# Softmax reciprocals of two batches taken once per head and spread by TensorE, in a fused attention and feed-forward kernel

## The chip, the core and the metric

The kernel runs on one core of a Trainium2 chip. A core has TensorE (PE in the profile; PEld is its loading of weights), VectorE (DVE), ScalarE (ACT), GpSimd (POOL) and SyncE (SP), each with its own instruction queue, and 16 DMA engines. Each queue runs in order. The metric is the device time of one execution in microseconds (us). Before the change the median of four runs is 249.94 us (248.99 to 250.69).

## The reference

The first half is Nyström attention over 8 batches and 8 heads, with 576 positions, 64 values per head and 32 landmarks (means over 18 positions). Three softmaxes are formed, the middle one is inverted by six steps of an iteration, and the product goes with v. The second half is a feed-forward layer with silu on the 4608 x 512 result.

```python
A  = sm(q, k_lm)          # 576 x 32 per head, each row divided by its sum
Bm = sm(q_lm, k_lm)       # 32 x 32
C  = sm(q_lm, k)          # 32 x 576
Z  = Bm.transpose(...) / (norms of Bm)
for _ in range(6):
    Z = 2 * Z - Z @ Bm @ Z
x  = A @ Z @ C @ v        # then heads side by side: 4608 x 512
h  = x @ w_in             # 512 -> 2048
out = (h * sigmoid(h)) @ w_out
```

## The kernel before

All work is cut into named operations ("A.1" is the product for softmax A of batch 1), each with its possible engines, an estimated duration, what it depends on, a priority and the number of PSUM banks it takes. A list scheduler (`Plan.run`) places them on the engines by these estimates; the instructions are then written out in that order and every engine runs its own list as it stands. The table `ORDER` shifts the priority of single operations. `margin` (0.4 us in general, `Plan.MARGIN`) is how long after its inputs are expected a PE operation is placed. In the first 45 us PE gets filler matmuls on a zero tile `zer` wherever the plan has nothing for it.

Heads stand in two groups g of four, with 4 x 32 landmarks on the 128 partitions, and positions in two halves c of 288. For one batch b:

- k and q are loaded (POOL queue), transposed (`tr`, by PE for batches 0 to 2, by DMA from SP for the others) and copied to `qT`; landmark sums (`lms`, `lm`, `lmT`), the small softmax (`sb`, `pb`) and the iteration (`f0`, six pairs `ns` on PE and `nsd` on DVE, tile `st`) follow.
- C: product C, Exp `Cx` on ACT with the row sums, transposes `ct`, product with v (`cv`), scaled `wsb`, then `zt`.
- m: `m0` to `m3`, the product of `zt` with a quarter (chunk) of `w_in` each, copied to `m`. So `w_in` is applied before A.
- A: product A into four banks; Exp (L786) to the bf16 tile `et`, 128 landmarks by 288 positions for each g and c; then the row sums. A matmul with `hmask` (`bones`, S) sums each head's 32 partitions and puts the sum on all 32. ACT takes Ln of it from PSUM (L796, four of 288 columns) and then Exp of minus that, in place (L800, two of 576 columns). DVE multiplies `et` with this reciprocal to `etn` (L805, two of 576).
- Layer 1 (`h0` to `h15`, and `hx0`, `hx8` for the last positions): product of `m` with `etn`, silu on ACT to `gm` and `gx`.
- Layer 2: `p1` to `p7`, a product scheme with seven instead of eight partial products, with sums on DVE; PSUM results are copied or added into `ost` by ACT and DVE (`c11`, `c12`, `c21`, `c22`) and stored by `os` operations.

ACT has two tables, one with Exp and Ln and one with silu; a switch is an instruction of its own. All table operations of one batch's softmaxes form a group, and silu is held back while a group is open. Silu of batch 0 also needs `pb` of batch 1, so the groups of batches 0 and 1 come before the first silu. C.1 and A.1 wait for `etn` of batch 0.

A tile of the result leaves in four stores of 64 KB, all on SP; only the last pair of tiles is split over SP and ACT, its second tile in halves of 256 columns.

Of the kernel before, what the change touches and what calls it, by code (L numbers as in the profile page):

```python
# [7 lines left out]
FP = mybir.dt.float32  # L8
# [8 lines left out]


ORDER = {
    "tr09.0": (11.858, 0), "f0.0": (2417.6, 0), "nsd20.0": (1178, 0), "stf1.0": (616.27, 0),  # L20
    "ns51.0": (572.47, 0), "A.0": (-14.244, 0), "Ax10.0": (-14.785, 0), "S10.0": (429.53, 0),
    "Ln10.0": (-9.5622, 0), "etn1.0": (303.1, 0), "mc00.0": (-3617.7, 0), "mc30.0": (2226.2, 0),
    "tr10.1": (11.49, 0), "trc09.1": (-0.41208, 0), "tr014.1": (4003.2, 0), "lms110.1": (600, 0),
    "lms1112.1": (182.03, 0), "lms006.1": (4219.8, 0), "ns00.1": (-205.63, 0),
    "Ax10.1": (-68.603, 0), "Ln10.1": (-2.9831, 0), "Ax11.1": (-215.55, 0),
    "Ln11.1": (-2436.1, 0), "Rs1.1": (-229.25, 0), "Cx00.1": (3739.9, 0), "ctc10.1": (-135.78, 0),
    "trc014.2": (-5.8828, 0), "Ln10.2": (-1553.1, 0), "Cx10.2": (-2.3811, 0), "h11.1": (3839, 0),
    "c12@5100.0": (-2978.9, 0), "A.3": (-178.57, 0), "cv0.3": (-11.245, 0), "h2.2": (332.83, 0),
    "h3.2": (185.78, 0), "h4.2": (18.041, 0), "h11.2": (452.76, 0), "h15.2": (51.328, 0),
    "p5@5200.0": (-179, 0), "c21@5200.0": (912.94, 0), "A.4": (-26.98, 0), "Ln00.4": (288.73, 0),  # L30
    "h11.3": (169.04, 0), "ss00@5320.0": (-3259.3, 0), "p5@5340.0": (-0.29183, 0),
    "p7@5340.0": (-4146.8, 0), "p3@5340.0": (212.88, 0), "nsd00.5": (-245.94, 0),
    "S10.5": (-942.67, 0), "p7@5420.0": (-0.18573, 0), "ns40.6": (267.98, 0),
    "ss00@5500.0": (-5226.2, 0), "cv0.7": (-3352.4, 0), "wrc.7": (1720.5, 0),
    "p5@5620.0": (-0.51334, 0), "p7@5700.0": (-1.908, 0), "p4@5720.0": (524.17, 0),
    "p2@5740.0": (15.37, 0),
}


# [264 lines left out]
def act_us(n):  # L304
    return 0.06 + 0.00083 * n
# [11 lines left out]
def kernel(  # L317
# [24 lines left out]
    SW = 128 + L  # L342
    NPE = 2
    NTR = 3
    SBF = 2
    MERGE = False
    WM = False
    NCT = 2
# [11 lines left out]
    def bank(o, i=0):  # L360
        return banks[o.slot[i]]
# [169 lines left out]
    def folds(e):  # L531
        for r in (0, 64):
            for c in (0, 64):
                nc.vector.tensor_copy(out=fold[r:r + 64, c:c + 64], in_=idb[r:r + 64, r:r + 64])
    cfold = A("fold", [("DVE", 0.6)], folds, [cid], 90.0)


# [6 lines left out]
    def attn(b):  # L544
# [225 lines left out]
        def am(e):  # L770
            for g in range(NG):
                for h in range(4):
# [5 lines left out]
                    lmT_all + ([] if cr else [(pb_op, -0.2)]) + qt_ops[0, 0] + qt_ops[0, 1] + ready, p0 + 20,  # L778
                    psum=4, tiled="q")
        me["A"].opens = grp  # L780
        for g in range(NG):
            et, ln = et_r[g], ln_r[g]
            lns = []
            for c in range(2):
                x = A(f"Ax{g}{c}.{b}", [("ACT", act_us(HS))],
                      lambda e, g=g, et=et, c=c: nc.scalar.activation(  # L786
                          out=et[:, c], in_=bank(me["A"], 2 * g + c)[:, 0:HS], func=AF.Exp,
                          scale=sc / J),
                      [me["A"], prev.get(f"etn{g}")], p0 + 21 + g, table="exp",
                      group=grp).reads(me["A"], 2 * g + c)  # L790
                me["S", g, c] = A(f"S{g}{c}.{b}", [("PE", mm_us(HS))],
                                  lambda e, g=g, c=c, et=et: mm(
                    bank(me["S", g, c])[:, 0:HS], bones, et[:, c]), [x, c0],
                    p0 + 22 + g, psum=1)
                lns.append(A(f"Ln{g}{c}.{b}", [("ACT", act_us(HS))],
                             lambda e, g=g, c=c, ln=ln: nc.scalar.activation(  # L796
                                 out=ln[:, c], in_=bank(me["S", g, c])[:, 0:HS], func=AF.Ln),
                             [me["S", g, c]], p0 + 25 + g, table="exp", group=grp).reads(
                                 me["S", g, c]))
            x = A(f"Rs{g}.{b}", [("ACT", act_us(S))], lambda e, ln=ln: nc.scalar.activation(  # L800
                out=ln, in_=ln, func=AF.Exp, scale=-1.0), lns, p0 + 25.1 + g, table="exp",
                group=grp)

            def etm(e, g=g, et=et, ln=ln):
                nc.vector.tensor_tensor(out=etn[:, g, :], in0=et.rearrange("p c x -> p (c x)"),  # L805
                                        in1=ln.rearrange("p c x -> p (c x)"), op=OP.mult)
            me[f"etn{g}"] = A(f"etn{g}.{b}", [("DVE", dve_us(S))], etm,
                              [x, l1_done.get(b - 2)], p0 + 30)
# [184 lines left out]
    def layer2_plain(gm, c, deps, places, prio):  # L993

        pieces = []
        for h in range(2):
            cell = {}
            cols = slice(c + 128 * h, c + 128 * h + 128)
            for qt in range(4):
                def f(e, qt=qt, cell=cell, cols=cols):  # L1000
                    for dc in range(4 * qt, 4 * qt + 4):
                        mm(bank(cell["o"]), gm[:, dc, cols], w_out_sb[:, dc, :], start=(dc == 0),
                           stop=(dc == NDC - 1))
                d = deps(4 * qt, 4 * qt + 4) + [wo_ops[qt]]
                o = A(f"o{qt}@{prio + h}", [("PE", mm_us(512, 4))], f,
                      d + ([(pieces[-1], 0.0)] if qt else []), prio + h + 0.01 * qt,
                      psum=0 if qt else 1, cls="L2")
                cell.setdefault("o", o)
                pieces.append(o)
            i = nost[0] % 6  # L1010
            nost[0] += 1
            t = ost_r[i]
            a = A(f"oc@{prio + h}", either(512), lambda e, t=t, cell=cell: copy(
                e, t, bank(cell["o"])), [pieces[-1]] + ost_st.get(i, []),
                500.0 + prio / 100).reads(cell["o"])
            ost_st[i] = [A(f"os@{prio + h}", [("SP", 2.2)],
                           lambda e, t=t, h=h: [store(e, t, places[h], m) for m in range(4)],
                           [a], prio, dma=0.65, lag=3.5)]
        return pieces
# [4 lines left out]
            out=out[b * S:(b + 1) * S, cols].rearrange("(l j) n -> j l n", j=J)[j],  # L1024
            in_=t[L * m:L * m + L, cols])

    def layer2_pair(gm, c, deps, places, prio, parts=1, spread=False):

        n = npair[0]
        npair[0] += 1  # L1030
# [74 lines left out]
        ss_last[n] = [p3, p5, p6]  # L1105

        for i, t, h, dep in ((lo_i, lo_t, 0, [c11, c12]), (hi_i, hi_t, 1, [c21, c22])):
            if spread and h:
                ost_st[i] = [A(f"os{u}{m}@{prio + h}", [("SP", 0.45), ("ACT", 0.45)],
                               lambda e, m=m, t=t, u=u: store(e, t, places[1], m, slice(  # L1110
                                   HM * u, HM * u + HM)), [dep[u]], prio + 0.1 * u,
                               dma=0.1, lag=1.5) for u in range(2) for m in range(4)]
            elif spread:
                ost_st[i] = [A(f"os{m}@{prio}", [("SP", 0.45), ("ACT", 0.45)],
                               lambda e, m=m, t=t: store(e, t, places[0], m), dep, prio,
                               dma=0.1, lag=1.5) for m in range(4)]
            else:
                ost_st[i] = [A(f"os@{prio + h}", [("SP", 2.2)],
                               lambda e, t=t, h=h: [store(e, t, places[h], m) for m in range(4)],
                               dep, prio, dma=0.65, lag=3.5)]  # L1120
        return pieces

    def layer2_batch(b):
        l2_last["m", b] = []
        for p in range(2):
            x = (gm_r[b % 2], 256 * p, lambda d0, d1: gm_ops[b][d0:d1],
                 [[(b, j) for j in range(8 * c + p, 8 * c + p + 7, 2)] for c in range(2)],
                 5000.0 + 100 * b + 20 * p)
            if b or p:
                l2_last["m", b] += layer2_pair(*x)  # L1130
            else:
                l2_last["m", b] += layer2_plain(*x)
                w_sums(l2_last["m", b][:])
        if b % 4 == 3:
            l2_last["x", b // 4] = layer2_pair(
                gx_t, 0, lambda d0, d1: [gx_ops[x][d // 8] for x in range(b - 3, b + 1)
                                         for d in range(d0 // 8 * 8, d1, 8)],
                [[(x, j) for x in (y, y + 1) for j in (J - 2, J - 1)] for y in (b - 3, b - 1)],
                5000.0 + 100 * b + 40, 1, b == B - 1)

    def later_loads(b):
        p = last[b - 2]
# [6 lines left out]
    for b in range(B + 1):  # L1149
        if b < B:  # L1150
            attn(b)
        if b:
            layer1(b - 1)
            layer2_batch(b - 1)

    order = P.run()
    if PLAN_DUMP is not None:
        PLAN_DUMP(order)
# [49 lines left out]
```

## Time and profile before

| What | us |
|---|---|
| median of four runs | 249.94 |
| the profiled execution | 250.13 |
| its span, first to last instruction | 247.5 |
| q of batch 0 landed, first half | 8.6 |
| softmax A, Ln of batch 0 begin on ACT | 15.99 |
| first Exp of softmax C of batch 1 on ACT | 23.03 |
| last filler on PE starts | 33.99 |
| layer 1 of batch 0: first and last silu end | 32.42 to 41.5 |
| last product of PE begins | 241.80 |

The page counts an engine's busy time from each instruction's start to its modelled end. The timeline gives the start, the length, the engine, the line and what was written from what; a bracket tells how long the engine stood idle before and what released it. Groups give the number of instructions, their busy time in us and the mean in ns. Times count from the start of the span.

### The profile page before, as it was taken

The page shows a single profiled execution, that of the slowest core. Times are in us where ns is not written, and L with a number is a line of the kernel's source. Part 1 is how long each engine was busy: PE and PEld are TensorE (multiplying, and loading weights), DVE is VectorE, ACT ScalarE, POOL GpSimd, SP SyncE. Part 2 cuts the span into 40 slices and gives each one's busy share as a digit, 9 for nine tenths or more (in the row PEclk, how much of TensorE's full clock was granted, in tenths as well). Part 3 has the DMA queues.
Part 4 walks back from the last instruction along what each step waited for, and adds up shares of the span by engine and source line. Part 5 has one row for each costly group of instructions (what it writes and reads, how often), then busy time and mean ns, then how long its engine had stood idle before and what let it go on. Part 6 is the DMA issues. An engine that isn't in the chain of part 4 may idle for free.

```text
span 247.5 us, 7085 instructions
## 1 busy us (share of the span) xinstructions
PE 239.9 (97%) x2780; PEld 171.6 (69%) x2780; DVE 168.6 (68%) x432; ACT 180.9 (73%) x443; POOL 37.2 (15%) x63
## 2 busy tenths in 40 slices
PE   8999999999989999999999999999999999999992
PEld 6886664566777655577886645697886665788881
DVE  2389765495989938939998777089988365056620
ACT  2596996499777999999259998868667998831220
POOL 8436733200022005000400050000000000000000
PEclk9999999999999999999999999999999999999999
DMA  6999999999979999999896999894344003032332
GB/s 104 203 198 196 203 207 206 206 242 160 166 140 229 183 145 183 217 154 170 152 244 175 182 169 226 142 155 111 86 119 103 6 3 85 3 85 66 97 95 85
DMA packets 55680, 36.50 MB, mean 147 GB/s; under 512 B 36576, under 2 KB 47072, under 8 KB 55648
## 3 DMA queue, kind: packets, MB, share of 16 engines
q0 software_dynamic: 15264, 18.35, 44.5%
q1 hardware_dynamic: 40096, 17.45, 32.9%
q8 instruction: 21, 0.34, 0.6%
q10 hardware_dynamic: 288, 0.26, 0.4%
q14 instruction: 11, 0.09, 0.1%
HBM read 36.70 MB, written 9.44 MB: 186 GB/s over the span
## 4 chain that ended last, share of the span: by engine, by line
PE 90%; DMA 4%; ACT 2%; DVE 1%; issue 1%; POOL 0%; DVEq 0%; ACTq 0%; POOLq 0%
PE ps L396 87%; DMA qk<-in_q_dram 2%; PE ps L570 2%; DMA qT<-qk 2%; ACT gm L958 1%; PE ps L846 1%; ACT L1161 1%; POOL qk L449 0%; DVE ost L1081 0%; ACT pb L695 0%; DVE red L630 0%; ACT gx L981 0%; ACT ost L406 0%; DVE st L756 0%; ACT zt L406 0%
## 5 line engine op out<-in xcount | busy, mean ns | idle before, releaser
L396 PE MATMUL ps<-etn,m 128*128 128x64 bf16 (+1 forms) x512 | 69.5, 286 | 0.6 <-ACT gm L958 0.6
L958 ACT ACTIVATE gm<-ps 128x512 f16<-128x512 f32 x128 | 66.7, 657 | 1.3 <-PE ps L396 1.0
L396 PEld LDWEIGHTS <-gm 128*128 128x128 f16 x512 | 48.6, 98 | 11.4 <-issue 2.7
L396 PE MATMUL ps<-w_out_sb,gm 128*128 128x256 f16 (+1 forms) x392 | 53.1, 281 | 0.0
L396 PEld LDWEIGHTS <-m 128*128 128x128 bf16 x512 | 32.2, 98 | 24.4 <-issue 2.7
L406 ACT COPY ost<-ps 128x256 f32<-128x256 f32 (+1 forms) x55 | 21.2, 388 | 37.1 <-PE ps L396 36.8
L396 PEld LDWEIGHTS <-ss 128*128 128x128 f16 x408 | 38.8, 98 | 8.0 <-issue 2.4
L1081 DVE TENSOR_TENSOR ost<-ost,ps 128x256 f32<-128x256 f32 x51 | 21.3, 418 | 31.1 <-PE ps L396 24.5
L396 PE MATMUL ps<-wt,ss 128*128 128x256 f16 x272 | 34.3, 273 | 0.7 <-DVE ost L1081 0.7
L756 DVE SCALAR_TENSOR_TENSOR st<-st,ps 128x320 bf16<-128x320 bf16 (+3 forms) x54 | 21.7, 407 | 7.7 <-PE ps L396 6.7
L408 DVE CAST m<-ps 128x512 bf16<-128x512 f32 x31 | 20.1, 686 | 3.2 <-PE ps L396 3.2
L406 ACT CAST m<-ps 128x512 bf16<-128x512 f32 x33 | 18.1, 616 | 2.0 <-PE ps L396 1.9
L396 PE MATMUL ps<-w_out_sb,ss 128*128 128x256 f16 x136 | 17.6, 273 | 0.0
L455 POOL DMA_DIRECT2D qk<-in_k_dram x7 | 5.0, 717 | 79.6 <-DMA ct<-ce 39.9
L396 PE MATMUL ps<-zer 128*128 128x256 bf16 x88 | 15.7, 306 | 1.1 <-DVE zer L489 1.1
L462 POOL DMA_DIRECT2D v<-in_v_dram x24 | 14.0, 591 | 16.7 <-PE ps L396 8.2
L396 PE MATMUL ps<-wt,gm 128*128 128x256 f16 x120 | 15.6, 273 | 0.0
L831 ACT ACTIVATE ce<-ps 128x288 bf16<-128x288 f32 x32 | 12.7, 417 | 3.2 <-PE ps L396 3.2
L396 PE MATMUL ps<-st 128*128 128x160 bf16 (+1 forms) x96 | 14.6, 225 | 0.1
L1046 DVE TENSOR_TENSOR ss<-gm 128x1024 f16<-128x1024 f16 x15 | 10.3, 684 | 4.9 <-ACT gm L958 4.9
L796 ACT ACTIVATE ln<-ps 128x288 f32<-128x288 f32 x32 | 12.0, 434 | 1.8 <-PE ps L396 1.6
L396 PEld LDWEIGHTS <-st 128*128 128x128 bf16 x96 | 8.5, 97 | 6.0 <-issue 1.1
(91 smaller groups left out, 323.5 us busy)
## 6 DMA issues: line engine op xcount, KB each, us to landing
out_dram<-ost SPq DMA_DIRECT2D x138, 64.0 KB, 1.8
v<-in_v_dram POOLq DMA_DIRECT2D x24, 192.0 KB, 10.9
qk<-in_k_dram POOLq DMA_DIRECT2D x7, 576.0 KB, 7.7
qk<-in_q_dram POOLq DMA_DIRECT2D x7, 576.0 KB, 10.7
w_out_sb<-in_moe_w_out_dram POOLq DMA_DIRECT2D x4, 512.0 KB, 11.0
w_in_sb<-in_moe_w_in_dram POOLq DMA_DIRECT2D x4, 256.0 KB, 9.2
w_in_sb<-in_moe_w_in_dram POOLq DMA_DIRECT2D x8, 128.0 KB, 7.6
qk<-in_k_dram POOLq DMA_DIRECT2D x2, 288.0 KB, 4.2
```

What stands on the lines that cost most here:

```text
L396: nc.tensor.matmul(out=out_ap, lhsT=lhsT, rhs=rhs, start=start, stop=stop, skip_group_check=True)
L406: nc.scalar.copy(out=out, in_=in_)
L408: nc.vector.tensor_copy(out=out, in_=in_)
L455: lambda e, t=t, src=src: nc.gpsimd.dma_start(out=qk_r[b % 2][:, t].rearrange("p g j d -> p g (j d)"), in_=src[b].rearrange("(g h) (l j) d ...
L462: lambda e, a=a: nc.gpsimd.dma_start(out=v_r[b % 2][a * L:(a + 1) * L, :, :], in_=v[b].rearrange("h (l a x) d -> a l h (x d)", l=L, a=VA)[ ...
L570: nc.tensor.transpose(out=ps[:, n * 128:(n + 1) * 128], in_=qk[:, t, g, 2 * jp:2 * jp + 2, :].rearrange("p j d -> p (j d)"), identity=idb)
L756: nc.vector.scalar_tensor_tensor(out=s2[:, g0:g1, lo:SW], in0=s[:, g0:g1, lo:SW], scalar=2.0, in1=ps[:, 0:NG * SW].rearrange("p (g x) -> p ...
L796: lambda e, g=g, c=c, ln=ln: nc.scalar.activation(out=ln[:, c], in_=bank(me["S", g, c])[:, 0:HS], func=AF.Ln),
L831: nc.scalar.activation(out=ce[:, :, 0:VP].rearrange("p (i c) (a l) -> p c a i l", c=2, a=VA)[:, c], in_=bank(me["C"], 2 * g + c)[:, 0:HS]. ...
L958: lambda e, dc=dc, cell=cell: nc.scalar.activation(out=gm[:, dc, :], in_=bank(cell["o"]), func=AF.Silu),
L1046: lambda e, o_=o_[:, k], x=x[:, k], y=y[:, k], op=op: nc.vector.tensor_tensor(out=o_, in0=x, in1=y, op=op), dep, 850.0 + prio / 100)
L1081: nc.vector.tensor_tensor(out=out_, in0=x, in1=y, op=OP.add)
```

## The change

For batches 0 and 1 (`NRC`) the row sums are handled once per head instead of once per landmark. Four matmuls with 32 output columns each (every fourth column of `bones`, so eight equal copies per head) put the sums of all g and c side by side on 128 partitions of one bank. One Ln (with scale 8) and one Exp of minus that, both of 288 columns, give an eighth of the reciprocal. It is split into a bf16 high part (`Rh`, a copy) and a low part (`Rl`, a subtraction on DVE). For every g and c two matmuls with a selecting matrix `sel` add the eight copies up, high and low part into one bank, so that the reciprocal stands on all 32 partitions of its head. DVE multiplies `et` with that bank to `etn`, in four instructions of 288 columns. `sel` is formed once, in the tile `red`, by a sum and a copy on DVE.

Besides, `margin` becomes 0.1 us (`EARLY`) for the PE operations of batch 0, for those of batch 1 other than `h`, `m`, `zt` and `cv`, and for the plain products of layer 2; the table `ORDER` has other entries, so operations of all batches stand in another order; and the stores of the last batch are spread over SP and ACT: whole rows for its main pairs, halves of 256 columns for both tiles of the last pair. The estimates for stores change as well.

```diff
+    EARLY = 0.1
+    NRC = (0, 1)
+    HILO = True
...
+    def sels(e):
+        nc.vector.reduce_sum(out=pbs_r[0][:, 0:8].rearrange("p a g -> p (a g)"),
+                             in_=idb.rearrange("p (a x) -> p a x", x=8), axis=AX.X)
+        nc.vector.tensor_copy(out=sel, in_=bc(
+            pbs_r[0][:, 0:8].rearrange("p (a c) g -> p a (c g)", c=2), L, 3))
...
+        if b in NRC:
+            rcp = ln_r[b % 2][:, 0]
+
+            def sm(e):
+                for g in range(NG):
+                    for c in range(2):
+                        r = L * (2 * g + c)
+                        mm(bank(me["S"])[r:r + L, 0:HS], bones[:, 0:128:4], et_r[g][:, c])
...
+            x = A(f"Ln00.{b}", [("ACT", act_us(HS))], lambda e: nc.scalar.activation(
+                out=rcp, in_=bank(me["S"])[:, 0:HS], func=AF.Ln, scale=8.0), [me["S"]]
...
+            x = A(f"Rs0.{b}", [("ACT", act_us(HS))], lambda e: nc.scalar.activation(
+                out=rcp, in_=rcp, func=AF.Exp, scale=-1.0), [x], p0 + 25.1, table="exp",
+                group=grp)
...
+            if HILO:
+                x = A(f"Rh.{b}", either(HS), lambda e: copy(e, rhl[:, 0], rcp), [x], p0 + 26)
+                x = A(f"Rl.{b}", [("DVE", dve_us(HS))], lambda e: nc.vector.tensor_tensor(
+                    out=rhl[:, 1], in0=rcp, in1=rhl[:, 0], op=OP.subtract), [x], p0 + 26)
...
+                        for u in range(2):
+                            mm(bank(me["R", g, c])[:, 0:HS], w, rhl[:, u], start=(u == 0),
+                               stop=(u == 1))
...
+                    me[f"etn{g}{c}"] = A(f"etn{g}{c}.{b}", [("DVE", dve_us(HS))],
+                                         lambda e, g=g, c=c: nc.vector.tensor_tensor(
+                        out=etn[:, g, HS * c:HS * c + HS], in0=et_r[g][:, c],
+                        in1=bank(me["R", g, c])[:, 0:HS], op=OP.mult),
...
-                l2_last["m", b] += layer2_pair(*x)
+                l2_last["m", b] += layer2_pair(*x, spread=int(b == B - 1))
...
-                5000.0 + 100 * b + 40, 1, b == B - 1)
+                5000.0 + 100 * b + 40, 1, 2 * (b == B - 1))
...
+    for o in P.ops:
+        if o.engs[0][0] == "PE" and (o.name[-2:] == ".0" or o.name[-2:] == ".1" and not
+                                     o.name.startswith(("h", "m", "zt", "cv"))):
+            o.margin = min(o.margin, EARLY)
```

## The prediction

> **What bounds the kernel now.** I read the page first: the shares, the slices, the clock row and the chain.
>
> ```profile
> span 247.5 us, 7085 instructions
> PE 239.9 (97%) x2780; PEld 171.6 (69%) x2780; DVE 168.6 (68%) x432; ACT 180.9 (73%) x443; POOL 37.2 (15%) x63
> ...
> PE   8999999999989999999999999999999999999992
> ...
> ACT  2596996499777999999259998868667998831220
> ...
> PEclk9999999999999999999999999999999999999999
> ...
> PE 90%; DMA 4%; ACT 2%; DVE 1%; issue 1%; POOL 0%; DVEq 0%; ACTq 0%; POOLq 0%
> ```
>
> TensorE (PE) carries the chain (90%), at full clock everywhere. But 97% "busy" counts 88 filler matmuls on `zer`, so I counted work instead. Eight matmuls of 256 columns take 1.04 us with 0.27 for the last, so they start 0.11 apart; 512 columns start 0.216 apart: 0.42 ns per column and 2 ns each. By that price the old instruction list holds 215.1 us of real matmuls. The windows on `zer` show where PE is not needed: 22 fillers in 8 to 20 us, 43 in 20 to 35, none later. **So three stages can give time: the start-up until the last filler (33.99 us), the few stalls of PE between 34 and 243, and the tail from the last product to 247.5.** In between each matmul added costs its length.
>
> The changed operations lie in the start-up, so I read the timeline there, ACT first, then POOL and PE.
>
> ```profile
> 29.96 0.43 ACT L796 ACTIVATE ln<-ps 128x288 f32<-128x288 f32 x1
> 30.43 0.68 ACT L800 ACTIVATE ln<-ln 128x576 f32<-128x576 f32 x1
> 31.13 1.28 ACT L958 ACT_TABLE_LOAD   x1
> 32.42 4.03 ACT L958 ACTIVATE gm<-ps 128x512 f16<-128x512 f32 x8
> ```
>
> From 23.03 to 41.5 us ACT has no gap. Its table switch and the first silu come right behind the last Ln and Exp of batch 1: these lines are the release of layer 1. A second release is the load of `w_in`:
>
> ```profile
> 21.33 0.59 POOL L473 DMA_DIRECT2D w_in_sb<-in_moe_w_in_dram  x1 [0.68 <-DMA w_in_sb<-in_moe_w_in_dram]
> ...
> 28.80 0.41 PE L396 MATMUL ps<-w_in_sb,zt 64*32 64x512 bf16 x8
> ...
> 30.66 0.41 PE L396 MATMUL ps<-w_in_sb,zt 64*32 64x512 bf16 x8
> ```
>
> The last pieces of chunks 1, 2 and 3 are issued at 17.46, 21.33 and 23.91 and take 7.5, 6.9 and 6.6 us to land (DMA view, windows of one issue each): 25.0, 28.2, 30.5. The products m2.0 and m3.0 start 0.6 and 0.2 behind theirs.
>
> **The change, part by part.** Prices come from these rows:
>
> ```profile
> L796 ACT ACTIVATE ln<-ps 128x288 f32<-128x288 f32 x32 | 12.0, 434 | 1.8 <-PE ps L396 1.6
> L805 DVE TENSOR_TENSOR etn<-et,ln 128x576 bf16<-128x576 bf16 x16 | 11.7, 753 | 0.1
> L800 ACT ACTIVATE ln<-ln 128x576 f32<-128x576 f32 x16 | 10.7, 708 | 0.1
> ```
>
> *ACT*, per batch 0 and 1: four Ln (1.32 in a row) and two Exp (1.28 in a row) go; one Ln (0.33), one Exp of half the length (0.4) and, for batch 0, the high-part copy (0.35, by the 0.37 of the 256-column `lmT` copy) come. 2.6 less 0.75 to 1.1: 1.5 to 1.9 us saved.
>
> *PE*, per batch: four S matmuls of 288 columns go (0.122 apart: 0.49). Eight R matmuls come (0.98), and four S products on 32 output columns each. No row shows this shape; if they run side by side like the 64x32 tiles they take 0.12 and a switch (the set at 64.53 takes 0.38 to the next start, 0.245 of it columns: 0.135), if one by one 0.49. I take side by side. Sum: 0.6 to 1.1 more per batch. The list agrees: real work rises from 215.1 to 216.3, before switches, and fillers fall from 88 to 72.
>
> *DVE*, per batch: two multiplies of 0.75 go; four of 288 columns with a PSUM operand come (0.42 for 256 columns in the `wsb` row, so 0.45 each), and the low part (0.42, batch 1 also the high part): +0.7 to +1.1. The two `sel` instructions cost about 0.8 before 6.65 us, where DVE idles 1.95 us; if that cover were gone, batch 0's transposed copies would be 0.8 later.
>
> *What moves.* The new order puts batch 0's `f0` and its iteration before batch 1's transposes, and A.1, S.1 behind m1.0 and m2.0 on PE. Walked through with the durations above:
> 1. DVE has some 35 instructions between f0.0 (14.4) and the last `qT` copy that C.1 needs; start to start they sum to 7.4 us: 21.8. C.1 runs at 22.0, its Exps from 22.2 (before: 23.03).
> 2. m1.0 now stands ahead of A.1 and waits for chunk 1 (25.0); with six fillers A.1 runs at 25.9, later than before. Behind the waiting m1.0 stand A.1, h0.0, m2.0; ACT waits for A.1.
> 3. m2.0 waits for chunk 2 (28.2); then 0.25, hx0.0 0.5, an iteration step 0.15, S.1 0.26: 29.4. Ln, Exp: 30.3. Table load 1.28: **first silu 31.6 instead of 32.42.** So of ACT's 3.4 us only 0.8 is left; the loads take the rest.
> 4. m3.0 at 30.5, eleven fillers and a step: last filler ends at 32.2, not 34.1. But 199.15 us of work stand behind it in the new list, 197.5 behind the old: 34.1 + 197.5 = 231.6 against 231.35. **Gain 0.25.**
>
> *The stall at 71 us.*
>
> ```profile
> 70.30 0.69 DVE L630 TENSOR_TENSOR red<-qT 128x1024 f16<-128x1024 bf16 x1 [1.03 <-DMA qT<-qk]
> ...
> 71.37 1.03 PE L396 MATMUL ps<-wt,ss 128*128 128x256 f16 x8 [0.68 <-DVE ost L1081]
> ```
>
> DVE waits for batch 3's transposes and PE for a bank behind it (0.85 beyond the matmul's length). Loads are back to back until then, so this moment stays. The old list has 162.4 us of work left there, the new one about 161.4: a group of 8 more is ahead of the waiting one. Arrival 70.9 (231.35, 0.9 lost to switches as before, less 161.4), release 71.37. **Gain now 1.0.** Late next: batch 3's exp group, whose score product moves from 75.58 to about 76.4; ACT then has two `ost` and one `m` copy fewer ahead of the table load (1.2 us), so the first silu of batch 2 comes 0.6 earlier and PE's 0.73 wait at 88.1 ends with the gain at 0.6 to 1.1. I keep 1.0.
>
> *Between 100 and 240* the order is reshuffled without new work. I found no stall above 0.25 us there outside tile switches, so I cost it 0, with 0.8 to either side.
>
> *The tail.*
>
> ```profile
> 241.80 1.04 PE L396 MATMUL ps<-w_out_sb,gx 128*128 128x256 f16 x8
> ...
> 242.88 0.42 DVE L1081 TENSOR_TENSOR ost<-ost,ps 128x256 f32<-128x256 f32 x1 [1.32 <-PE ps L396]
> 242.91 1.87 SPq L1023 DMA_DIRECT2D out_dram<-ost  x4
> ```
>
> Behind the last add (243.3) stand four stores of 64 KB: ACT issues two at once, SP, busy with the other tile until 244.0, the last at 244.36; it lands at 246.17. Afterwards both tiles go in half-width stores, and behind the last copy only two are left per queue: issues at 243.35 and 243.75, landing 1.5 later (32 KB median): 245.25. **Gain 0.9.** The Trainium skill ("DMA: Bandwidth & Descriptors", Issuing engines are not separate DMA queues) speaks against it: all queues share the 16 engines, so spreading saves only sequencer time, usually small. By that alone it is worth 0 to 0.3; the row shows that here sequencer time (0.36 to 0.47 per store) is what ends last, so I take 0.9.
>
> *Fewer fillers.* "TensorE: Matmul & The Clock Gate" (What's actually happening) says that about 3.4 us without PE activity halve the clock. One such window at half clock would cost 1.7 us. The clock row never drops, and the longest stretch of waiting that I find in the new list (m1.0) is under 1 us with fillers around: cost 0; 1.7 is kept for the upper end.
>
> **Sum:** 1.0 + 0.9 = 1.9 off the profiled run's 250.13 (span 247.5 and 2.6 around it): 248.2. It lies 0.2 above the median of 249.94, so 248.0.
>
> **Rivals.**
> - *Only the tail counts (249.1).* PE's added work (1.2 to 1.5) eats the start-up's gain and PE meets the 71 us stall as before. For: fixed load times. Against: one more group ahead of the wait.
> - *ACT's saving comes through (246.2).* If S.1 and A.1 were not held by the loads, silu could start 2.5 us earlier, 1.8 beyond mine, nearly all of which PE could use. For: ACT without a gap from 23.03. Against: m1.0 and m2.0 stand ahead.
> - *DVE becomes the bound (250.6, slower).* Batch 0's iteration, four multiplies and batch 1's copies share one DVE queue from 14.4. Each iteration step also waits for PE behind blocks of 6 to 18 transposes (0.2 to 0.5). If the twelve steps lose 0.25 each, C.1 runs at 25.0, and past 0.5 us of slack (A.1's wait for chunk 1) all follows one for one: +2.5, so 250.5. It decides from C.1 at 24.4 (1.9 lost beyond the slack). Against: old DVE showed 0.2 us of waits for PE on these steps.
> - That the shortened softmax isn't there is excluded: the list shows one Ln and one Exp in both batches.
>
> **How the numbers follow.** Forecast 248.0: chance 0.55, own spread 1.2. Only the tail: 0.16. ACT's saving through: 0.20. DVE bound: 0.09. The range reaches from the third case's 246.2, less 0.4 for the later stages, to 250.1, which leaves most of the slower case out: 245.8 to 250.1. No change means within 0.5% (1.25 us, about what a measurement of this kernel can tell): 248.7 to 251.2. Faster: 0.45 of the forecast's 0.55, all 0.20, 0.05 of the tail case: 0.70. Slower: 0.06. Same: 0.24.
>
> **What would show it.** First silu near 31.6, the last filler near 32.2, m1.0 and m2.0 right behind their loads; PE's wait near 71 us under 0.5; some 1.9 us between the last DVE copy's end and the last landing instead of 2.9. Wrong if S.1 runs long before 28 us (third case), if DVE is without a gap until after 23 (slower case), or if new waits above 0.5 us show between 100 and 240.

## The result, and the profile after

The changed kernel takes 248.84 us (median of 44 runs, 247.72 to 250.8) against 249.85 for the kernel before (63 runs, 248.61 to 252.19): ratio 0.9961, 95% interval 0.9947 to 0.9975. So it is faster, by 1.0 us or 0.4%. That is less than the 0.5% that the prediction took as its bound for a change, so by its own classes the outcome is "no change" (its chance 0.24) and not "faster" (0.70). The median is 0.84 above the forecast of 248.0.

The lines of the page that answer to those shown of before:

```profile
span 248.7 us, 7113 instructions
PE 239.9 (96%) x2780; PEld 171.7 (69%) x2780; DVE 171.8 (69%) x442; ACT 181.3 (73%) x437; POOL 37.3 (15%) x63
...
PE   8899999999999999999999999999999999999991
...
PEclk9999999999999999999999999999999999999999
...
PE 81%; ACT 6%; DMA 5%; DVE 4%; issue 1%; POOL 0%; DVEq 0%; ACTq 0%; SPq 0%; POOLq 0%
```

This one execution has a span of 248.7, longer than before's 247.5, although the median is shorter: its last six stores took 3.2 to 3.5 us to land. A second profiled execution (run "again" below) has 247.0, and I compare that one where the end matters. PE is as busy as before and at full clock. Its share of the chain fell from 90% to 81%, and ACT's rose from 2% to 6%: the chain now steps to ACT and DVE more often, so waits of another kind have come in.

The new operations, in the groups kept apart by shape (count, busy us and mean ns, idle before):

```profile
L813 ACT ACTIVATE ln<-ps 128x288 f32<-128x288 f32 x2 | 0.8, 420 | 0.4 <-PE ps L398 0.4
L816 ACT ACTIVATE ln<-ln 128x288 f32<-128x288 f32 x2 | 0.9, 446 | 0.0
L839 DVE TENSOR_TENSOR etn<-et,ps 128x288 bf16<-128x288 bf16 x8 | 3.3, 449 | 0.3 <-ACT gm L1017 0.3
L398 PE MATMUL ps<-et,hmask 128*32 128x288 bf16 x8 | 0.6, 311 | 0.0
```

The prices hold: Ln 0.42, Exp 0.45, the multiply from PSUM 0.45. The four sums on 32 columns each take 0.32 us together (the timeline below), so they do run side by side.

The start-up of the changed kernel in the timeline (start, length, engine, line, operation):

```profile
28.23 0.41 PE L398 MATMUL ps<-w_in_sb,zt 64*32 64x512 bf16 x8
29.28 0.32 PE L398 MATMUL ps<-et,hmask 128*32 128x288 bf16 x4
29.68 0.41 ACT L813 ACTIVATE ln<-ps 128x288 f32<-128x288 f32 x1 [0.39 <-PE ps L398]
30.59 1.28 ACT L1017 ACT_TABLE_LOAD   x1
31.79 0.82 PE L398 MATMUL ps<-zer 128*128 128x256 bf16 x6
31.88 1.58 ACT L1017 ACTIVATE gm<-ps 128x512 f16<-128x512 f32 x3
32.53 1.08 PE L398 MATMUL ps<-etn,m 128*128 128x512 bf16 x4
```

The product m2.0 starts right behind chunk 2 (landed at 28.12), S.1 follows a microsecond later, Ln 0.4 after it, and the first silu comes at 31.88 (forecast 31.6, before 32.42). The last filler starts at 32.33 and so ends near 32.4 (forecast 32.2). The product m1.0, forecast to wait for chunk 1, starts at 25.76, 1.1 us behind its landing (24.64).

All waits of PE over 0.15 us between 55 and 96 us, changed kernel:

```profile
65.20 0.44 PE L398 MATMUL ps<-qT,lmT 64*32 64x288 bf16 x16 [0.46 <-ACT pb L707]
74.73 0.86 PE L398 MATMUL ps<-v,ct 96*64 96x128 bf16 x24 [0.23 <-DVE st L768]
85.70 0.41 PE L398 MATMUL ps<-w_in_sb,zt 64*32 64x512 bf16 x8 [0.39 <-ACT m L408]
89.65 1.57 PE L398 MATMUL ps<-etn,m 128*128 128x512 bf16 x6 [0.19 <-ACT gm L1017]
```

The 0.68 at 71.37 is gone, as forecast. But the brackets add up to 1.27 us, and before the two in this stretch (0.68 at 71.37, 0.57 at 88.10) made 1.25. In place of one stall stand several smaller ones with other releasers.

A bracket counts only the time past the modelled end of the matmul before it. Counted from start to start, less the price of each matmul, the stretch from 75 to 95 us loses 3.1 us in both traces of the changed kernel and 2.1 before. The lines of before that answer to it:

```profile
75.58 0.27 PE L396 MATMUL ps<-lmT 128*128 128x128 bf16 x2
83.26 0.84 PE L396 MATMUL ps<-w_in_sb,zt 64*32 64x512 bf16 x24
85.01 0.41 PE L396 MATMUL ps<-w_in_sb,zt 64*32 64x512 bf16 x8
88.10 1.11 PE L396 MATMUL ps<-etn,m 128*128 128x512 bf16 x18 [0.57 <-ACT gm L958]
```

and two more of the changed kernel:

```profile
77.67 0.28 PE L398 MATMUL ps<-lmT 128*128 128x128 bf16 x2
86.58 0.41 PE L398 MATMUL ps<-w_in_sb,zt 64*32 64x512 bf16 x8
```

In this count the changed kernel waits 0.46 at 85.70, 0.35 at 89.65, 0.21 at 88.18 and 0.19 at 78.94, together 1.21 us, against 0.73 at 88.10 before. The rest is spread over small steps; one is that the products of m on 64x32 tiles stand in three blocks where before they stood in two. The score product of batch 3 (the `lmT` lines) runs 2.1 us later than before.

The end of the changed kernel, second execution:

```profile
242.09 2.74 ACTq L1082 DMA_DIRECT2D out_dram<-ost  x6
242.25 1.04 PE L398 MATMUL ps<-wt,gx 128*128 128x256 f16 x8
243.32 0.42 DVE L410 COPY ost<-ps 128x256 f32<-128x256 f32 x1 [0.45 <-PE ps L398]
```

The last copy ends at 243.75, the last store is issued at 244.39 and lands at 246.05: from PE's last matmul to the end of the span 3.74 us, where before had 4.70. That is 0.96 us, about the whole measured gain. Every other trace with the new softmax, order and stores has 3.73 to 3.75 there; only the first profile, with its late landings, has 5.37. By the medians too PE ends no earlier: the spans of "again" (247.7 before, 246.6 changed, medians) less these 4.70 and 3.74 give 243.0 and 242.9.

Of the 0.96 only 0.57 lies where the prediction put it, between the last copy and the last landing: 2.87 us before, 2.30 now. The other 0.39 comes behind the last landing, where the closing instructions take 1.37 us in before and 0.98 in "again"; why is open.

To see what PE itself gained I kept the prediction's account: a moment plus the real matmuls still ahead at it, by the same price. The landing of the first half of q.0 is taken off, since it lies between 8.1 and 9.1 us from one execution to the next. Where the number grows, PE has lost time.

| moment | before | same PE list (`tail_only`) | changed (again) | changed, no late fillers | before, no late fillers |
|---|---|---|---|---|---|
| 35 us | 222.97 | 223.0 | 223.04 | 222.57 | 222.51 |
| 75 us | 225.54 | 225.1 | 225.36 | 224.62 | 224.51 |
| 95 us | 227.70 | 227.3 | 228.54 | 227.67 | 226.72 |
| 155 us | 231.35 | 230.2 | 231.66 | 231.14 | 230.54 |
| 235 us | 234.05 | 233.0 | 234.27 | 233.75 | 233.25 |

The changed kernel is level at 35, 0.2 ahead at 75, 0.8 behind at 95 and 0.2 behind at the end. Each column is one execution, and one column shows how far that can be trusted: `tail_only` (below) has the PE list of before up to 233.9 us, yet the two differ by up to 1.2. Against it the changed kernel is not ahead at 75 and 1.2 to 1.5 behind from 95 on. What holds in every comparison is that the changed kernel gains 0.2 at most up to 75 us and loses about 1 between 75 and 95. For the whole the medians below decide.

### The profile page after: what moved, and what is told of

Same layout as the page of the kernel before. It is cut to its first block, busy times and chain, and to the rows that moved or that the text cites. A ratio compares the mean times of both kernels' runs of the same rounds, so it can differ in the third digit from the quotient of the medians.

```text
span 248.7 us, 7113 instructions
## 1 busy us (share of the span) xinstructions
PE 239.9 (96%) x2780; PEld 171.7 (69%) x2780; DVE 171.8 (69%) x442; ACT 181.3 (73%) x437; POOL 37.3 (15%) x63
## 4 chain that ended last, share of the span: by engine, by line
PE 81%; ACT 6%; DMA 5%; DVE 4%; issue 1%; POOL 0%; DVEq 0%; ACTq 0%; SPq 0%; POOLq 0%
PE ps L398 79%; ACT gm L1017 3%; DMA qk<-in_q_dram 3%; DMA qT<-qk 2%; PE ps L582 2%; DVE m L410 1%; ACT m L408 1%; ACT pb L707 1%; DVE etn L864 1%; PE ps L905 1%; ACT L1224 1%; DVE red L642 0%; POOL qk L451 0%; DVE st L768 0%; DVE ost L410 0%
## 5 line engine op out<-in xcount | busy, mean ns | idle before, releaser
L1017 ACT ACTIVATE gm<-ps 128x512 f16<-128x512 f32 x128 | 65.8, 647 | 0.9 <-PE ps L398 0.4
L408 ACT COPY ost<-ps 128x256 f32<-128x256 f32 (+1 forms) x51 | 19.8, 389 | 39.4 <-PE ps L398 36.2
L410 DVE CAST m<-ps 128x512 bf16<-128x512 f32 x30 | 19.6, 685 | 1.6 <-PE ps L398 1.3
L410 DVE COPY ost<-ps 128x256 f32<-128x256 f32 x19 | 8.0, 423 | 12.8 <-PE ps L398 11.7
L398 PE MATMUL ps<-zer 128*128 128x256 bf16 x72 | 12.3, 313 | 1.1 <-DVE zer L491 1.1
## 6 DMA issues: line engine op xcount, KB each, us to landing
w_out_sb<-in_moe_w_out_dram POOLq DMA_DIRECT2D x4, 512.0 KB, 10.6
```

The lines of the kernel that those rows point to most:

```text
L398: nc.tensor.matmul(out=out_ap, lhsT=lhsT, rhs=rhs, start=start, stop=stop, skip_group_check=True)
L408: nc.scalar.copy(out=out, in_=in_)
L410: nc.vector.tensor_copy(out=out, in_=in_)
L1017: lambda e, dc=dc, cell=cell: nc.scalar.activation(out=gm[:, dc, :], in_=bank(cell["o"]), func=AF.Silu),
```

## The experiments

My theory after the result was: the tail is the whole gain, and what the start-up gives PE is used up by new waits between 63 and 95 us. Rivals: the added matmuls eat it; the fillers matter; the softmax or the order of issue is what pays. Medians, and ratios to the kernel before on the same chip:

| run | us (runs) | ratio, 95% interval |
|---|---|---|
| again (changed kernel) | 248.77 (17) | 0.9967, 0.9948 to 0.9985 |
| tail_only | 249.70 (14) | 0.9993, 0.9974 to 1.0011 |
| no_tail | 250.72 (9) | 1.0044, 1.0024 to 1.0065 |
| no_low | 248.35 (12) | 0.9946, 0.9923 to 0.9970 |
| s1_early | 249.08 (22) | 0.9977, 0.9959 to 0.9994 |
| no_late_fill | 248.41 (20) | 0.9953, 0.9934 to 0.9972 |
| old_softmax | 259.36 (6) | 1.0385, 1.0351 to 1.0419 |
| before_new_order | 256.76 (6) | 1.0289, 1.0258 to 1.0319 |
| exp3_early | 248.56 (22) | 0.9948, 0.9927 to 0.9969 |
| before_no_late_fill | 248.87 (22) | 0.9976, 0.9955 to 0.9996 |
| s1_nofill | 248.04 (14) | 0.9946, 0.9928 to 0.9964 |
| all_edits | 248.97 (13) | 0.9966, 0.9948 to 0.9985 |

**The changed kernel once more.**

> The changed kernel once more, for a second profile. Its first profile had its last stores landing 3.4 us after their issue, where the prediction and the kernel before have 1.5. If that belongs to one execution only, this profile shows 1.5 to 2.0 us and a span near 247; if it belongs to the new store pattern, it shows about 3.4 again. Time near 248.8 either way.

It gave 248.77.

**The stores alone, and all but the stores.** `tail_only` is before with the new stores of the last batch; `no_tail` is the changed kernel with the old ones, the reverse of this diff (shown where the stores are asked for):

```diff
-                l2_last["m", b] += layer2_pair(*x)
+                l2_last["m", b] += layer2_pair(*x, spread=int(b == B - 1))
...
-                5000.0 + 100 * b + 40, 1, b == B - 1)
+                5000.0 + 100 * b + 40, 1, 2 * (b == B - 1))
```

> The kernel before with nothing but the spread stores of the last batch. If the tail is worth what the prediction says, 0.9 us less than before (249.0 against 249.9) with the last landing about 1.9 us after the last copy; if the change's gain is all tail, 1.0 less; if spread stores collide, no gain.

> The changed kernel with the stores of the last batch as before; TensorE's order is the same. If the prediction's split holds (1.0 from start-up and the stall at 71 us, 0.9 from the tail), 1.0 less than before. Rival, that the new softmax and order give nothing in sum: as before (249.9), within 0.3.

The stores alone gave nothing (249.70 beside 249.7), all but the stores cost 1.0 us, and in the new order the stores are worth 250.72 less 248.77: 1.95 us. Neither edit moves stores alone, since the scheduler plans anew around them: in `tail_only` PE's list differs from 233.9 us on and three copies move from ACT to DVE, in `no_tail` PE's list is the same and two copies move from DVE to ACT. The timelines say why. `tail_only`:

```profile
239.39 5.32 ACTq L1023 DMA_DIRECT2D out_dram<-ost  x10
242.38 0.42 DVE L408 COPY ost<-ps 128x256 f32<-128x256 f32 x1 [0.45 <-PE ps L396]
```

Here the last five copies end 0.82 to 0.88 us apart (239.36 to 242.80), and the two stores per queue that each of them releases take ACT and SP about 0.8. ACT's queue issues ten stores in 5.3 us with one pause of 0.6, SP's is as busy, and the last issue comes at 244.28, 1.48 after the last copy's end; in the changed kernel, whose queues stand idle from 240.3 to 242.1, it is 0.64. `no_tail`:

```profile
237.08 9.69 SPq L1082 DMA_DIRECT2D out_dram<-ost  x13
240.97 0.42 DVE L1140 TENSOR_TENSOR ost<-ost,ps 128x256 f32<-128x256 f32 x1 [2.20 <-DMA out_dram<-ost]
241.43 4.20 ACTq L1082 DMA_DIRECT2D out_dram<-ost  x7
```

Here the new order meets the old queues: DVE waits for a tile to be stored before it may write it again, SP is still issuing at 246.35, 3.3 us after the last copy, and the end of the span comes 6.45 after PE. So the gain belongs to neither part by itself. It takes an order that has one tile out of the way early and queues that keep up with it. PE's old list to its end with the new stores wasn't measured.

**The low part's matmuls.** They are 0.98 of PE's 1.2 us of added work.

```diff
-                        for u in range(2):
-                            mm(bank(me["R", g, c])[:, 0:HS], w, rhl[:, u], start=(u == 0),
-                               stop=(u == 1))
+                        mm(bank(me["R", g, c])[:, 0:HS], w, rhl[:, 0])
```

> The changed kernel without the product of the low bf16 part (8 matmuls of 288 columns fewer in all, 0.98 us of TensorE; the reciprocals have bf16 precision). The order is the same. If added matmul work costs its length as the prediction holds, 0.8 to 1.0 less than the changed kernel; if the start-up's waits and the later waits on ScalarE and loads hide it, less than 0.3.

248.35 is 0.4 below the changed kernel, between the two expectations, and the intervals overlap: undecided. In its one trace the PE account at 85 us was no lower than the changed kernel's: up to there the matmuls that went had become waiting.

**An earlier first silu.**

```diff
+    place(take([f"Ax{g}{c}.1" for g in range(2) for c in range(2)]), "A.1", 1)
+    place(take(["S00.1", "Ln00.1", "Rs0.1"]), "m2.0", 0)
+    order = [(x[0], "DVE") + x[2:] if x[0].name in ("mc20.0", "mc21.0") else x for x in order]
```

> The changed kernel with three things of the issue order edited by hand: batch 1's first softmax Exps stand right behind its score product A.1 on ACT, its denominators (S.1, Ln, Exp) stand just ahead of the layer-1 product m2.0 and not behind it, and both copies of m2.0 go to VectorE. Nothing computed differs. From the trace of the changed kernel the first silu should start about 0.7 us earlier (31.15 us where it was 31.9). Theory 1 (what the start-up gains is used up before 95 us by waits on ACT, VectorE and loads, so PE's end does not follow the first silu): within 0.3 us of the changed kernel's 248.8, so 248.5 to 249.0. Rival (the first silu sets the end one for one): 248.0 to 248.2.

249.08: no gain. The timeline of this kernel shows that my reading of it was too simple:

```profile
29.59 1.28 ACT L1017 ACT_TABLE_LOAD   x1
30.79 0.59 PE L398 MATMUL ps<-etn,m 128*128 128x512 bf16 x2 [0.40 <-DVE st L768]
30.89 1.57 ACT L1017 ACTIVATE gm<-ps 128x512 f16<-128x512 f32 x3
32.49 0.82 PE L398 MATMUL ps<-zer 128*128 128x256 bf16 x6
33.15 1.03 PE L398 MATMUL ps<-etn,m 128*128 128x512 bf16 x4
33.78 1.60 ACT L1017 ACTIVATE gm<-ps 128x512 f16<-128x512 f32 x3 [1.32 <-PE ps L398]
```

The silu comes 0.4 to 1.1 us earlier than in the five traces of the changed kernel's start-up (31.24 to 32.00), but PE is held for an iteration step and then runs eleven fillers that stand in its list ahead of h3.0 (six are shown); ACT, early for once, waits 1.32 us for PE. A filler is planned into a gap that the plan expects. When the gap isn't there, it is work.

**No late fillers,** in the changed kernel (28 left out), in the kernel before (44 by the count in its trace, 88 to 44; the 30 of the expectation is wrong), and together with the earlier silu (`s1_nofill`):

```diff
-    order = P.run()
+    order = [x for x in P.run() if x[0] is not P.filler or x[2] < 20.0]
```

> The changed kernel without the 28 filler matmuls on zer that its list holds after 20 us (some 3 us of PE time); all else in the same order. Theory 1 (fillers stand only where PE waits anyway, and the clock does not need them): 248.5 to 249.1, granted clock full. Rival A (fillers delay what stands behind them): 248.0 to 248.4, with the last product of layer 1 of batch 0 (h3.0 and on) earlier. Rival B (they keep the clock up): a stretch at lower granted clock after 20 us and 250.0 to 250.8.

> The kernel before without the 30 filler matmuls on zer that its list holds after 20 us; all else in the same order. In the changed kernel the same edit gave about 0.4 us. Theory 1 (the kernel before meets its stall at 71 us, which hangs on the transposed loads, whatever happens in the start-up): within 0.3 us of before, 249.3 to 249.8. Rival (the fillers delay the start-up and the start-up sets the end in the old order as well): 0.4 to 0.9 us faster, 248.7 to 249.2.

> The changed kernel with both edits at once: batch 1's softmax Exps and denominators further ahead, and no fillers after 20 us. In s1_early the first silu came some 0.7 us earlier but the layer-1 product h3.0 stood behind fillers on PE and came no earlier. Theory 1 (once the fillers are gone the first silu does release PE): first silu near 30.6 us, h3.0 near 31.4, and 0.2 to 0.7 us less than without the fillers alone (248.4), so 247.7 to 248.2. Rival (the iteration steps on VectorE, which stall PE for 0.4 us there, or waits at 63 to 90 us take it up): 248.3 to 248.8.

The changed kernel gained about 0.4 (248.41), within the intervals of each other. The kernel before gained 0.85 by the medians and 0.6 by the ratio (whose interval lies below 1), against my theory: **without its late fillers the kernel before, with the old softmax, the old order and the old stores, is as fast as the changed kernel** within what these runs can tell (248.87 and 248.84, the intervals of the ratios overlap). In windows of `no_late_fill` (busy us and count of each engine, then PEclk, DMA share, GB/s) the clock stays full:

```profile
20.00:26.00 6.00, 5.29 (x112) 3.53 (x110) 5.73 (x23) 5.35 (x16) 3.73 (x6) 1.00 1.24 203
26.00:35.00 9.00, 7.72 (x87) 4.18 (x80) 7.01 (x18) 7.88 (x17) 5.04 (x8) 1.00 1.24 206
```

PE is busy for 13.0 of 15 us there, not all 15, and PEclk reads 1.00. And in `before_no_late_fill` the stall at 71 us is gone:

```profile
69.57 0.69 DVE L630 TENSOR_TENSOR red<-qT 128x1024 f16<-128x1024 bf16 x1
70.27 0.65 PE L396 MATMUL ps<-et,hmask 128*128 128x288 bf16 x4
70.76 1.04 PE L396 MATMUL ps<-wt,ss 128*128 128x256 f16 x8
```

No bracket: batch 3's last transpose landed at 69.45 instead of 70.17. In the four traces without late fillers it lands between 68.8 and 69.5, in the ten with them between 70.2 and 71.2. I had called this moment fixed by the loads; it isn't, though why the fillers should bear on it stays open. Nor is the stall fixed in a kernel that keeps its fillers. In `tail_only`, with the same PE list up to there, it is a third of what it is in before:

```profile
71.42 1.03 PE L396 MATMUL ps<-wt,ss 128*128 128x256 f16 x8 [0.23 <-DVE ost L1081]
```

PE came 0.5 us later there (q.0 landed at 9.11, in before at 8.61), and the transposes at the same time (70.22). So a part of the stall that the prediction set out from belonged to one execution. `s1_nofill` has the lowest median of all, 248.04; its interval still overlaps that of the changed kernel, so it is likely, not shown, that it is faster.

**Old softmax under the new order, and the new order alone.** `old_softmax` is the changed kernel with `NRC = ()`; `before_new_order` is before with the other table `ORDER`.

> The changed kernel with the old denominators in batches 0 and 1 (four sums over 128 output rows, four Ln and two Exp per batch, one multiply per head pair; no low and high parts), with the new table for the issue order and the new spread of the last batch's stores. PE has 1.0 to 1.2 us less real work and ACT some 3.5 us more in the start-up. Theory 1 (the softmax itself is worth about nothing, since its gain on ACT is met by PE's added work and by waits behind it; the tail makes the change): 248.3 to 249.5, and a first silu within 0.8 us of the changed kernel's. Rival (the new softmax is what pays): 249.8 to 251, with a first silu more than 1 us later than the changed kernel's.

> The kernel before with nothing changed but its table for the issue order, for which the changed kernel's table is put in; old softmax, old stores. The table is fitted to the costs of the kernel that it belongs to. Theory 1 (the middle of the list, 60 to 240 us, is neither better nor worse by more than a few tenths under the new table, and the old stores cost it up to 1.8 us as they did in the changed kernel): 250 to 252. Rival (the new table is what makes the changed kernel faster): 248.5 to 249.3.

Both fell far outside every expectation: 10.6 us above the changed kernel, and 7.2 above before. The timeline of `old_softmax`:

```profile
30.95 1.28 ACT L1017 ACT_TABLE_LOAD   x1
...
196.03 1.28 ACT L1224 ACT_TABLE_LOAD   x1
...
202.82 1.28 ACT L1017 ACT_TABLE_LOAD   x1
204.76 1.50 PE L398 MATMUL ps<-etn,m 128*128 128x512 bf16 x4 [1.95 <-ACT gm L1017]
```

Most of the harm, 8.4 us by the PE account, is at 195 to 215 us, where no operation of batches 0 and 1 stands: ACT switches its table twice within 7 us, with the softmaxes of a late batch in between, and PE waits for the silu behind. The table is a set of nudges to one plan; for other operations the same nudges give a plan that nobody chose. So these two can't tell what the softmax or the order is worth by itself. Up to 85 us, however, `old_softmax` can be read: its first silu is at 32.24, in the five traces with the new softmax and this start-up at 31.24 to 32.00, so ACT's longer softmax costs 0.2 to 1.0 us there, and its account at 85 us is level with the changed kernel's (226.66 and 226.54). The new softmax with the old table, or a table made anew for the old softmax, wasn't measured.

**Batch 3's group.** `exp3_early` moves its score product, `all_edits` also the product C.3 and, besides, has the edits of `s1_nofill`:

```diff
+    place(take(["ltr0.3"]), "cv0.2", 0)
+    place(take(["sb.3"]), "p5@5120.0", 0)
+    place(take(["pb.3"]), "c21@5100.0", 0)
...
+    place(take(["A.3"]), "p2@5120.0", 0)
+    place(take(["pbs.3", "pbr.3"]), "nsd30.2", 0)
...
+    place(take(["C.3"]), "p7@5120.0", 0)
+    place(take(["Cx00.3", "Cx01.3", "Cx10.3", "Cx11.3"]), "C.3", 1)
```

> The changed kernel with one part of the issue order edited by hand: batch 3's score chain (the second fold of the landmark sums, the landmark score sb.3, the score product A.3 and its sums S.3 on PE, with pb.3 on ACT and its four small VectorE steps) stands one to two blocks of eight matmuls further ahead, about where the kernel before had it. In the trace of the changed kernel A.3 ran at 78.88 us (before 76.87) and the first silu of batch 2 at 88.45 (before 87.45). Theory 1 (this late group is what costs the changed kernel its early gain between 80 and 95 us): A.3 near 77.6, first silu of batch 2 near 87.4, and 0.4 to 0.9 us less than the changed kernel, 247.9 to 248.4. Rival (the waits there come from VectorE's and ACT's total work, whatever the order): other waits appear and 248.6 to 249.2.

> The changed kernel with the edits of s1_nofill and, on top, batch 3's whole group further ahead in the issue order: score product A.3 with its four Exps and sums S.3 as in exp3_early but in the right sequence on ACT, and also the read-out product C.3, one block of eight matmuls earlier. In exp3_early A.3 came 1.5 us earlier, but C.3 stayed at 82.4 us and the first silu of batch 2 with it, and PE's waits at 85 and 89 us (0.5 and 0.35) stayed. Theory 1 (C.3 and the copies behind it on ACT set the first silu of batch 2, and this is where the changed kernel loses between 80 and 95 us): first silu of batch 2 some 0.5 us or more earlier against the landing of q.0, the waits at 85 and 89 us gone or halved, and 0.3 to 0.8 us less than s1_nofill, 247.3 to 247.8. Rival (the order there is bound by VectorE and ACT together): new waits of the same size, 247.9 to 248.4.

In `exp3_early` the first of batch 3's sums is formed ahead of its Exps, from the data of batch 2, and ACT waits 0.97 us for it. A part of batch 3 is thus divided by sums that are not its own and the output is not that of the reference; the run counts for its order and its time only. The rest stands as meant. A.3 came 1.5 us earlier, the waits at 85 and 89 us stayed, and 248.56 is near the rival's figure. `all_edits` puts that right and has C.3 earlier too:

```profile
81.54 0.65 PE L398 MATMUL ps<-qT,lmT 64*32 64x288 bf16 x16 [0.28 <-DVE pbs L727]
85.15 1.07 ACT L408 CAST m<-ps 128x512 bf16<-128x512 f32 x2 [1.29 <-PE ps L398]
88.59 2.06 ACT L1017 ACTIVATE gm<-ps 128x512 f16<-128x512 f32 x4
```

ACT is done with batch 3's softmax C 1.5 us sooner (83.6, in "again" 85.1) and then waits 1.29 us for the products m of batch 2, so the first silu is no earlier (88.59; 88.45 in "again"), and PE has two new waits (0.28 at 81.5 and 0.29 at 83.7 by the brackets). 248.97 is 0.9 more than `s1_nofill` by the medians, with intervals that overlap. My theory that batch 3's group alone holds the first silu of batch 2 falls: with the group out of the way, m of batch 2 holds it at the same moment. What holds m, I take it, is the iteration of that batch on PE and DVE, two queues that everything else here uses too; no run shows that.

## Why the prediction was right in part

- **Sign and range:** right, but the range is 4.3 us wide, the gain is half of the 1.9 forecast, and it stays under my own bound for a change. It lies behind PE's last product alone, and the rival "only the tail counts" (249.1, chance 0.16) describes the result better than my forecast (248.0, 0.55).
- **The softmax's prices, S.1 held by chunk 2, first silu at 31.6, last filler at 32.2:** right (31.88 and 32.4). Chunk 1 did not hold m1.0 (1.1 us behind it); A.1 came a microsecond late all the same, as C.1 had. ACT's saving did not come through in PE's end, as I had argued against that rival: in `old_softmax` its absence costs the first silu 0.2 to 1.0 us and nothing in the account at 85. DVE did not become the bound either: C.1 ran at 23.0, not past 24.4.
- **Start-up, gain 0.25:** measured about 0 (222.97 and 223.04), within what one trace can tell. C.1 ran at 23.0 instead of 22.0, behind the last copies of `qT` on ACT and DVE (22.8), and A.1 at 26.9 instead of 25.9. What I missed is the price of the fillers, which I had counted as idle time: leaving them out is worth 0.6 to 0.85 us in the kernel before and perhaps 0.4 in the changed one.
- **The stall at 71 us, "gain now 1.0", and batch 3, "I keep 1.0":** this is the step that failed. I took one wait away and let the gain stand, having named one wait that could be late next. In the trace PE has 0.2 of the 1.0 at 75 us (none of it against `tail_only`, where the old stall is 0.23), and at 95 it is 0.8 behind. The waits are 0.46 for `pb`, 0.23 for `st`, 0.39 for `m` and 0.19 for `gm`. The first silu of batch 2, which I put 0.6 us earlier, came 1.0 later (87.45 to 88.45). ACT's work did shrink: from batch 3's first Exp for A to the table load it takes 7.9 us where it took 8.9. But this group starts 2.0 later (77.25 to 79.26), since the score product, which the forecast with PE a microsecond ahead put at 76.4, ran at 77.67.
- **100 to 240 us at 0 within 0.8:** the table shows 0.6 regained (0.84 behind at 95, 0.22 at the end), but before's one trace is itself slower here than `tail_only` with the same list, against which nothing is regained. No PE wait that the profile lists stands there.
- **The tail, 0.9:** 0.96, the size right with some luck. From the last copy to the last landing it is 0.57 (2.30 us, forecast 1.9), and 0.39 behind the landing were in no forecast. Its ground was incomplete too: I credited the stores, and without the new order they give nothing. The Trainium skill's rule ("DMA: Bandwidth & Descriptors", Issuing engines are not separate DMA queues), that spreading saves only sequencer time, fits `tail_only`; in the new order the sequencer's time was what ended last, and was worth 1.95.
- **Fewer fillers cost the clock nothing:** right, even with none after 20 us.

## What to carry to other kernels

A stall that one trace shows may be that execution's own, so look at it in a second one before crediting it. When a stall is taken away, sum the waits of the whole stretch behind it for the new order before crediting the gain, and ask of each engine what it will wait for, not only how much work it has. In a list that is written out in advance, fillers are instructions like any other: if the moment behind them can come earlier, they are what holds it, so try the kernel without them before changing anything else. A table of priorities is fitted to one set of operations; don't read an operation's worth from a kernel that keeps the table of another.

## What was not expected of the hardware

Of the DMA transposes issued between 61 and 69 us, about 1.4 us apart, one or two take 4.1 to 5.3 us from issue to landing where most others take 3.3 to 3.6. In the changed kernel it is the fourth of `qT` (65.81 to 70.94); without late fillers it is one of `ct`, and the four of `qT` are through 1.5 to 2.2 us sooner. And in the profiled execution of the changed kernel the last stores, issued from 243.4 on, needed 3.2 to 3.5 us to land, where they took about 1.6 in "again" (244.39 to 246.05) on the same instructions.
